# An exp without its wait for the older exp, an early flag and branch hints in a fused attention and FFN kernel

One core of a Trainium2 chip. The metric is the device time of the kernel in microseconds (us), lower is better. All outputs are checked against the reference. Engines: PE is TensorE, DVE VectorE, ACT ScalarE, POOL GpSimd, SP SyncE. A semaphore is what one engine updates and another waits for when a result is ready; the records hold the times of its updates. "The kernel before" and "the changed kernel" are the two versions compared.

## The reference

Multi-query attention (32 heads of 16, one K and V for all) on a normalized input, times a gate made by an FFN, plus the input. S = 2048, D = 512, F = 1792, bfloat16.

```python
xn = _layernorm(x, axis=-1)
# A: q = xn@wq (32 heads), k = xn@wk, v = xn@wv
scores = jnp.einsum("bhqd,bkd->bhqk", q, k) * (Dh ** -0.5)
p = _softmax(scores, axis=-1)
s = (jnp.einsum("bhqk,bkd->bhqd", p, v) ...) @ wo
# B:
g = _silu((_silu(xn @ w_gate) * (xn @ w_up)) @ w_down)
return x + s * g
```

## The kernel before

The body is a static schedule. PE makes a 128x1024 tile of scores into one of three PSUM buffers (`ring`). The exp is taken by ACT for most of the tiles and by DVE, in several operations, for the others; PE multiplies the result with V. ACT writes its exps into eight buffers `Pb` in turn. The exp written into a buffer now must come after the products that read its former content, and these come after the exp that wrote it:

```python
    NPB = 8
    Pb = [sb([P, 1024], BF16, f"Pb{i}") for i in range(NPB)]
    # ... (cut)
    def act_sc(i, b, x, start, dur=MMF):
        # ... (cut: places the score products sc of this tile, and picks k, the number of the exp)
            buf = Pb[k % NPB][:]
        ex = OP("ACT", 0.904, [sc, pb_rel[k - NPB] if k >= NPB else None, cur["exp"]],
                lambda: nc.scalar.activation(out=buf, in_=ring[i][:], func=ACT.Exp, scale=escale, bias=ebias),
                (1,), name="exp")
        # ... (cut: pb_rel[k] becomes the product on PE that reads the buffer)
```

The kernel takes the softmax without a maximum. At the end it tests whether all denominators lay in range; if not, a branch computes everything again by an exact path. With ordinary data the branch skips that path (it is taken). The end of the kernel, with the last four row tiles of the output:

```python
    tadd("DVE", e_out_mul(LN, obk[0], dsts[0]))
    fin_add(0, nc.gpsimd, "POOL")
    # ... (cut: three more products and additions)
    for k in range(4):
        tadd("SP", e_out_st(LN + k))
    tadd("DVE", nc.vector.tensor_reduce(out=fmin[:, 2:3], in_=dlc[:], axis=AX.X, op=ALU.min))
    tadd("DVE", nc.vector.tensor_reduce(out=fmin[:, 3:4], in_=fmin[:, 0:3], axis=AX.X, op=ALU.min))
    tadd("PE", nc.tensor.matmul(out=tq01[0:1, 0:1], lhsT=fmin[:, 3:4], rhs=ones_f[:], start=True, stop=True))
    tadd("DVE", nc.vector.tensor_single_scalar(out=flag_i[:], in_=tq01[0:1, 0:1], scalar=P - 0.5, op=ALU.is_lt))
    MAIN.close()

    flag = nc.values_load(flag_i[0:1, 0:1], min_val=0, max_val=1)
    with tc.If(flag > 0):
        _exact_max_path(...)
```

`tadd(engine, instruction)` appends to the order of an engine. `values_load` loads the flag into a register of every engine, because every engine branches (the trace has five loads of 472 to 539 ns, at 775.05 to 775.06 us, and five branches).

Of the kernel before, what the change touches and what calls it, by code (L numbers as in the profile page):

```python
# [13 lines left out]
ACT = mybir.ActivationFunctionType  # L14
ALU = mybir.AluOpType
AX = mybir.AxisListType
# [3 lines left out]
P = 128  # L20
# [263 lines left out]
def kernel(  # L284
# [13 lines left out]
    nc = tc.nc  # L298
# [8 lines left out]
    escale = LN2 / GRID  # L307
    ebias = -COFF * LN2
# [18 lines left out]
    flag_i = const.tile([1, 1], I32, name="flag_i")  # L327
# [22 lines left out]
    def sb(shape, dtype, name):  # L350
        return wp.tile(shape, dtype, name=name)

    ring = [psum.tile([P, 1024], FP32, name=f"ring{i}") for i in range(3)]
# [20 lines left out]
    NPB = 8  # L374
# [17 lines left out]
    dlc = sb([P, 32], FP32, "dlc")  # L392
    fmin = sb([P, 4], FP32, "fmin")
    ones_f = sb([P, 1], FP32, "ones_f")
# [3 lines left out]
    _last = {}  # L398

    def chain(eng, ins):  # L400
        for bi in (ins if isinstance(ins, (list, tuple)) else [ins]):
            if eng in _last:
                tc.add_manual_dep(bi.ins, _last[eng].ins.name, _nosync, reason="order")
            _last[eng] = bi
# [8 lines left out]
    for c in range(1, NSC):  # L413
# [12 lines left out]
                                        in_=wk_sb[:].rearrange("p k (o d) -> p k o d", o=1).to_broadcast(  # L426
                                            [P, KC, 8, DH])))
# [4 lines left out]
    for i in range(NWARM):  # L432
        chain("PE", nc.tensor.matmul(out=ring[2][:, 512:1024], lhsT=ident_bf[:], rhs=QB[1][:],  # L433
                                     start=True, stop=True))
# [52 lines left out]
    def cmm(dst, w, rhs, start, stop):  # L487
        return [nc.tensor.matmul(out=dst[GRP * j:GRP * j + GRP, :], lhsT=w[:, GRP * j:GRP * j + GRP], rhs=rhs,  # L488
                                 start=start, stop=stop, tile_position=(0, GRP * j)) for j in range(P // GRP)]
# [4 lines left out]
    def OP(eng, dur, deps, emit, prio, mode=None, name=""):  # L494
        return sd.new(_Op(eng, dur, deps, emit, prio, mode, name))
# [118 lines left out]
    for c in range(1, NSC):  # L614
# [4 lines left out]
                name="kev")  # L619
# [62 lines left out]
    def e_out_mm(n, dst, jjs):  # L682
        qs, tt = n // 4, n % 4
        r = []
        for jj in jjs:
            r += cmm(dst, oT[qs % 2][:, jj, tt * P:(tt + 1) * P], wo_sb[:, jj, :], jj == 0, jj == NQ - 1)
        return r

    def e_out_mul(n, src, dst):
        return nc.vector.scalar_tensor_tensor(out=dst[:, :D], in0=src, scalar=0.25, in1=g2_sb[:, n, :],  # L690
                                              op0=ALU.mult, op1=ALU.mult)

    def e_out_add(n, src, eng):
        r = res[n % 4]
        return eng.tensor_tensor(out=r[:, :D], in0=src[:, :D], in1=x_sb[:, n, :] if n >= LN else r[:, :D], op=ALU.add)

    def e_out_st(n):
        return nc.sync.dma_start(out=out_v[:, n, :], in_=res[n % 4][:, :D])
# [39 lines left out]
    def pv_emit(b, mms):  # L738
        for (_, _, g) in mms:
            pv_total[(b, g)] = pv_total.get((b, g), 0) + 1  # L740

        def f():
            r = []
            for (lhs, rhs, g) in mms:
                n = first_pv.get((b, g), 0)
                first_pv[(b, g)] = n + 1
                r.append(nc.tensor.matmul(out=o_ps[GRP * g:GRP * g + GRP, :], lhsT=lhs, rhs=rhs,  # L747
                                          start=(n == 0), stop=(n == pv_total[(b, g)] - 1),
                                          tile_position=(0, GRP * g)))
            return r  # L750
        return f
# [35 lines left out]
    cur = {"ba": 0, "lastx": 1, "nA": 0, "exp": None, "pair": None, "np": 0, "issued": 0, "lastsc": None, "junk": 0, "nX": 0, "pa": None}  # L787
    slot = [None, None, None]
    pb_rel = []
# [30 lines left out]
    def act_block():  # L820
        b = cur["ba"]
        while b < NBLK and rem(b, 0) + rem(b, 1) == 0:
            b += 1
        return b if b < NBLK else None
# [58 lines left out]
    def mm_of(lhs_of, buf, t, half, gs):  # L883
        return [(lhs_of[:, t, DH * half:DH * half + GRP], buf(g), g) for g in gs]
# [14 lines left out]
    def check_done(b):  # L899
        if nx[b][0] == NT and nx[b][1] == NT and not (cur["pair"] is not None and cur["pair"][0] == b):  # L900
            assert not unp[b][0] and not unp[b][1]
            fin_b.add(b)
            kb_ready[b] = cur["lastsc"]
            finish_block(b)

    def place_sc(sl, b, x, start, dur):
        ensure_open(b)
        t = take(b, x)
        ks = k_ready[t // 4][b % 2]
        ks = ks[t % 4 // 2:t % 4 // 2 + 1] if len(ks) > 1 else ks  # L910
        sc = _Op("PE", dur, [slot[sl]] + ks + q_ready[b // 2], sc_emit(sl, b, t, x), (0,), "r", "sc")
        sc.seq = sd.seq
        sd.seq += 1
        sd.place(sc, start)
        cur["lastsc"] = sc
        return sc, t

    act_q = []

    def act_sc(i, b, x, start, dur=MMF):  # L920
        sc, t = place_sc(i, b, x, start, dur)
        cur["lastx"] = x
        pre = b == 1 and cur["ba"] == 0 and act_block() == 0
        if pre:
            k = -1 - cur["nX"]
            buf = XB[cur["nX"]]
            cur["nX"] += 1
        else:
            cur["ba"] = b
            k = cur["nA"]  # L930
            cur["nA"] += 1
            buf = Pb[k % NPB][:]
            pb_rel.append(None)
        if k >= NPB:
            assert pb_rel[k - NPB] is not None
        ex = OP("ACT", 0.904, [sc, pb_rel[k - NPB] if k >= NPB else None, cur["exp"]],
                lambda: nc.scalar.activation(out=buf, in_=ring[i][:], func=ACT.Exp, scale=escale, bias=ebias),  # L937
                (1,), name="exp")
        cur["exp"] = ex
        act_q.append(ex)  # L940
        if len(act_q) > 8:
            act_q.pop(0)
        slot[i] = ex
        unp[b][x].append((ex, k, t, buf))
        if unp[b][0] and unp[b][1]:
            half = b % 2
            mms, dps, ks = [], [], []
            for xx in range(2):
                e_, k_, t_, b_ = unp[b][xx].pop(0)
                mms += mm_of(VA, lambda g, b_=b_: b_[:, (g % 2) * 512:(g % 2 + 1) * 512], t_, half,  # L950
                             (2 * xx, 2 * xx + 1))
                dps += [e_, v_ready[t_ // 4][0]]
                ks.append(k_)
            pv = OP("PE", MMF, dps + [oev[b - 1]], pv_emit(b, mms), (1, b, min(ks)), "c", "pv")
            blk_pv[b].append(pv)
            for k_ in ks:
                if k_ >= 0:
                    pb_rel[k_] = pv
        check_done(b)
        return sc  # L960
# [265 lines left out]
    def pe_do(start, what):  # L1226
# [44 lines left out]
        if dt is None:  # L1271
            act_sc(i, b, act_x(b), start)
            return
# [42 lines left out]
    def tadd(eng, ins):  # L1316
        chain(eng, ins)
# [4 lines left out]
    tq01, tq23 = ring[lb][:, 0:512], o_ps[:]  # L1322
# [14 lines left out]
    dlf = dl[:].rearrange("p h q g o -> p (h q g o)")  # L1337
    tadd("DVE", nc.vector.tensor_scalar(out=dlc[:], in0=dlf, scalar1=DEN_LO, scalar2=DEN_HI, op0=ALU.max, op1=ALU.min))
    tadd("DVE", nc.vector.tensor_tensor(out=dlc[:], in0=dlc[:], in1=dlf, op=ALU.is_equal))
    dsts = [ab[0], ab[1], oa[(LB + 1) % 4], oa[(LB + 2) % 4]]  # L1340
    obk = [bank[k][:, :D] for k in st["obank"]]
    for k in range(2):
        tadd("PE", e_out_mm(LN + k, obk[k], [NQ - 1]))
    for k in range(2, 4):
        tadd("PE", e_out_mm(LN + k, obk[k], [NQ - 1]))

    def fin_add(k, eng, nm):
        tadd(nm, e_out_add(LN + k, dsts[k], eng))

    tadd("DVE", e_out_mul(LN, obk[0], dsts[0]))  # L1350
    fin_add(0, nc.gpsimd, "POOL")
    tadd("DVE", e_out_mul(LN + 1, obk[1], dsts[1]))
    tadd("DVE", e_out_mul(LN + 2, obk[2], dsts[2]))
# [3 lines left out]
    fin_add(3, nc.vector, "DVE")  # L1357
    for k in range(4):
        tadd("SP", e_out_st(LN + k))
    tadd("DVE", nc.vector.tensor_reduce(out=fmin[:, 2:3], in_=dlc[:], axis=AX.X, op=ALU.min))  # L1360
    tadd("DVE", nc.vector.tensor_reduce(out=fmin[:, 3:4], in_=fmin[:, 0:3], axis=AX.X, op=ALU.min))
    tadd("PE", nc.tensor.matmul(out=tq01[0:1, 0:1], lhsT=fmin[:, 3:4], rhs=ones_f[:], start=True, stop=True))
    tadd("DVE", nc.vector.tensor_single_scalar(out=flag_i[:], in_=tq01[0:1, 0:1], scalar=P - 0.5, op=ALU.is_lt))
    MAIN.close()


    flag = nc.values_load(flag_i[0:1, 0:1], min_val=0, max_val=1)
    with tc.If(flag > 0):
        _exact_max_path(tc, nc, wo_sb, x_v, out_v, wq_sb, xnT, KT, VA, g2_sb, ident_bf, ident_f, qscale,
                        S, D, H, NT, NQ, NSC, HD)  # L1370

# [29 lines left out]
```

## Time and profile before

| | kernel before |
|---|---|
| median of 3 runs | 783.76 us (783.62 to 784.1) |
| profiled span | 780.9 us, 21436 instructions |
| granted TensorE clock, mean share of full speed | 0.994 |
| last store issued / landed | 774.27 / 775.98 us |
| end of the records | 780.93 us |

The span is the stretch that has records. The measured time is longer, here by 1.8 to 3.4 us; no record shows what fills the rest. In the groups of instructions (line, engine, operation, tile, shape, count | busy us, mean ns of one | idle time of the engine just before and what ended most of it), this is the exp:

```profile
L937 ACT ACTIVATE Pb<-ring 128x1024 bf16<-128x1024 f32 x772 | 726.4, 1141 | 2.5 <-PE ring L877 2.3
```

The 772 exps fill 726.4 of 780.9 us, and ACT was idle before them for only 2.5 us in all. Their mean is 1141 ns.

### The profile page before, as it was taken

The page shows a single profiled execution, that of the slowest core. Times are in us where ns is not written, and L with a number is a line of the kernel's source. Part 1 is how long each engine was busy: PE and PEld are TensorE (multiplying, and loading weights), DVE is VectorE, ACT ScalarE, POOL GpSimd, SP SyncE. Part 2 cuts the span into 40 slices and gives each one's busy share as a digit, 9 for nine tenths or more (in the row PEclk, how much of TensorE's full clock was granted, in tenths as well). Part 3 has the DMA queues.
Part 4 walks back from the last instruction along what each step waited for, and adds up shares of the span by engine and source line. Part 5 has one row for each costly group of instructions (what it writes and reads, how often), then busy time and mean ns, then how long its engine had stood idle before and what let it go on. Part 6 is the DMA issues. An engine that isn't in the chain of part 4 may idle for free.

```text
span 780.9 us, 21436 instructions
## 1 busy us (share of the span) xinstructions
PE 749.8 (96%) x9095; PEld 230.2 (29%) x9095; DVE 735.7 (94%) x920; ACT 757.2 (97%) x866; POOL 53.5 (7%) x59
## 2 busy tenths in 40 slices
PE   8999999999999999999999999999999999999994
PEld 3323223322222333322232322222223333222221
DVE  7689999999999999999999999999999999999994
ACT  6999999999999999999999999999999999999992
POOL 2100000000012000000001110000000300000101
PEclk9999999999999999999999999999999999999997
DMA  9400000000001000000000100000000000000001
GB/s 329 139 8 9 16 2 24 2 8 17 6 27 49 24 2 8 17 2 24 3 10 29 42 23 2 24 1 9 17 2 24 29 22 2 3 23 2 23 2 32
DMA packets 21199, 20.20 MB, mean 26 GB/s; under 512 B 8744, under 2 KB 17192, under 8 KB 21096
## 3 DMA queue, kind: packets, MB, share of 16 engines
q1 hardware_dynamic: 19512, 18.20, 7.7%
q8 instruction: 73, 1.20, 0.6%
q10 hardware_dynamic: 1584, 0.56, 0.3%
q14 instruction: 30, 0.25, 0.1%
HBM read 14.19 MB, written 2.34 MB: 21 GB/s over the span
## 4 chain that ended last, share of the span: by engine, by line
PE 46%; ACT 38%; issue 8%; DVE 6%; SPq 0%; DMA 0%; ACTq 0%; POOL 0%; DVEq 0%; POOLq 0%
ACT Pb L937 33%; PE ring L877 17%; PE m_ps L488 15%; PE o_ps L747 13%; ACT th L657 3%; DVE Bf L991 2%; ACT g_sb L937 1%; DVE Bf L1010 1%; PE ring L433 1%; ACT th L674 1%; DVE x_sb L1010 0%; DVE x_sb L1005 0%; PE ring L488 0%; DVE hT L663 0%; DVE Bf L1005 0%
## 5 line engine op out<-in xcount | busy, mean ns | idle before, releaser
L937 ACT ACTIVATE Pb<-ring 128x1024 bf16<-128x1024 f32 x772 | 726.4, 1141 | 2.5 <-PE ring L877 2.3
L877 PE MATMUL ring<-QB,KT 32*128 32x512 bf16 x2048 | 306.1, 382 | 15.5 <-ACT Pb L937 8.9
L991 DVE TENSOR_SCALAR Bf<-ring 128x1024 uint16<-128x1024 f32 x172 | 209.6, 1218 | 5.4 <-PE ring L877 4.0
L877 PEld LDWEIGHTS <-KT 32*128 32x128 bf16 x2048 | 94.4, 91 | 314.1 <-issue 307.4
L747 PE MATMUL o_ps<-Pb,VA 128*32 128x512 bf16 x1544 | 146.9, 385 | 0.0
L1010 DVE TENSOR_TENSOR Bf<-Bf,Bf 128x2048 f16<-128x2048 f16 x74 | 90.3, 1220 | 0.1
L991 DVE TENSOR_SCALAR x_sb<-ring 128x1024 uint16<-128x1024 f32 x72 | 87.7, 1218 | 2.5 <-PE ring L877 2.1
L747 PE MATMUL o_ps<-xnT,zw 128*32 128x512 bf16 x1092 | 83.1, 381 | 0.0
L488 PE MATMUL m_ps<-xnT,wu_sb 128*32 128x512 bf16 x896 | 72.6, 384 | 0.8 <-DVE ab L659 0.6
L488 PE MATMUL m_ps<-wd_sb,hT 128*32 128x512 bf16 x896 | 71.5, 383 | 0.1
L488 PE MATMUL m_ps<-xnT,wg_sb 128*32 128x512 bf16 x896 | 70.4, 384 | 0.0
L747 PE MATMUL o_ps<-Bf,VD 128*32 128x512 f16 x688 | 67.1, 385 | 0.9 <-DVE Bf L1010 0.5
L732 POOL TENSOR_TENSOR oT<-oa,rb 128x512 bf16<-128x512 f32 x15 | 22.0, 1464 | 615.6 <-DMA rb<-dscr 409.2
L1017 DVE TENSOR_SCALAR Bf<-Bf 128x2048 uint16<-128x2048 uint16 x86 | 62.0, 721 | 0.6
L747 PEld LDWEIGHTS <-VA 128*32 128x32 bf16 x1560 | 38.0, 94 | 53.8 <-issue 51.5
L1005 DVE TENSOR_SCALAR Bf<-Bf 128x2048 uint16<-128x2048 uint16 x74 | 51.2, 700 | 0.0
L659 DVE SCALAR_TENSOR_TENSOR ab<-th,m_ps 128x512 f32<-128x512 f32 x56 | 38.1, 681 | 4.2 <-ACT th L657 3.9
L657 ACT ACTIVATE th<-m_ps 128x512 f32<-128x512 f32 x56 | 40.1, 716 | 0.0
L663 DVE TENSOR_TENSOR hT<-ab,m_ps 128x512 bf16<-128x512 f32 x56 | 38.2, 682 | 2.0 <-PE m_ps L488 1.6
L747 PEld LDWEIGHTS <-VD 128*32 128x32 f16 x976 | 26.5, 94 | 39.4 <-issue 35.8
L747 PEld LDWEIGHTS <-zw 128*32 128x32 bf16 x1092 | 25.8, 95 | 25.5 <-issue 12.9
L1010 DVE TENSOR_TENSOR x_sb<-x_sb 128x2048 f16<-128x2048 f16 x24 | 29.2, 1217 | 0.0
(121 smaller groups left out, 416.3 us busy)
## 6 DMA issues: line engine op xcount, KB each, us to landing
rb<-dscr SPq DMA_DIRECT2D x15, 256.0 KB
out_dram<-xn SPq DMA_DIRECT2D x16, 128.0 KB, 1.9
dn<-oa SPq DMA_DIRECT2D x120, 2.0 KB, 1.7
oa<-oa SPq DMA_DIRECT2D x60, 32.0 KB, 2.0
wg_sb<-in_B_w_gate_dram SPq DMA_DIRECT2D x1, 1792.0 KB, 11.5
wu_sb<-in_B_w_up_dram SPq DMA_DIRECT2D x1, 1792.0 KB
wd_sb<-in_B_w_down_dram SPq DMA_DIRECT2D x1, 1792.0 KB, 20.3
x_sb<-in_A_x_dram SPq DMA_DIRECT2D x3, 512.0 KB
```

Of the source, the lines that this page charges most:

```text
L488: return [nc.tensor.matmul(out=dst[GRP * j:GRP * j + GRP, :], lhsT=w[:, GRP * j:GRP * j + GRP], rhs=rhs, start=start, stop=stop, tile_posi ...
L657: t_ = OP("ACT", 0.477, [a], lambda: nc.scalar.activation(out=th[i][:], in_=m_ps[:], func=ACT.Tanh, scale=0.5), (0,), name="tanh")
L659: s_ = OP("DVE", 0.6, [t_, ab_rel[i]], lambda: nc.vector.scalar_tensor_tensor(out=ab[i][:], in0=th[i][:], scalar=1.0, in1=m_ps[:], op0=ALU ...
L663: h = OP("DVE", 0.6, [b], lambda: nc.vector.tensor_tensor(out=hT[:, f, :], in0=ab[i][:], in1=m_ps[:], op=ALU.mult), (1,), name="hmul")
L732: return [pk, q], lambda eng: eng.tensor_tensor(out=oT[qs % 2][:, jj, :], in0=o0[:], in1=rbt[:], op=ALU.mult)
L747: r.append(nc.tensor.matmul(out=o_ps[GRP * g:GRP * g + GRP, :], lhsT=lhs, rhs=rhs, start=(n == 0), stop=(n == pv_total[(b, g)] - 1), tile_ ...
L877: return lambda: [nc.tensor.matmul(out=ring[sl][:, u * 512:(u + 1) * 512], lhsT=KT[half][GRP * g:GRP * g + GRP, t * P:(t + 1) * P], rhs=QB ...
L937: lambda: nc.scalar.activation(out=buf, in_=ring[i][:], func=ACT.Exp, scale=escale, bias=ebias),
L991: lambda: nc.vector.tensor_scalar(out=U[:, hs], in0=ring[si][:], scalar1=ubias, scalar2=UINF, op0=ALU.add, op1=ALU.min), (1.5, u), name="p ...
L1005: o1 = OP("DVE", 0.6, [pa, pa0] + wrel, lambda: nc.vector.tensor_scalar(out=Bf[wi], in0=U, scalar1=0x3FF, scalar2=0x3800, op0=ALU.bitwise_and,
L1010: return lambda: eng.tensor_tensor(out=Bf[wi][:, a:z].bitcast(FP16), in0=Bf[wi][:, a:z].bitcast(FP16), in1=U[:, a:z].bitcast(FP16), op=ALU ...
L1017: o2 = OP("DVE", 0.6, o3, lambda: nc.vector.tensor_scalar(out=U, in0=U, scalar1=0x7C00, scalar2=None, op0=ALU.bitwise_and), (2, u, 1), nam ...
```

## The change

Three parts. (a) An exp is no longer told to wait for the exp eight earlier, because its wait for the products on PE implies it. (b) The flag is computed and loaded before the last output products, not after the last store. (c) Each engine gets a branch hint ahead of the closing branch. In the kernel before, ACT, DVE, PE and SP go on only 2.7 to 4.1 us after their branches, and four instruction fetches (three of 8 KB, one of 16 KB, at 776.5 to 776.9 us) lie in that stretch; the hope was that a hint brings such fetches forward.

```diff
-        ex = OP("ACT", 0.904, [sc, pb_rel[k - NPB] if k >= NPB else None, cur["exp"]],
-                lambda: nc.scalar.activation(out=buf, in_=ring[i][:], func=ACT.Exp, scale=escale, bias=ebias),
-                (1,), name="exp")
+        def emit():
+            bi = nc.scalar.activation(out=buf, in_=ring[i][:], func=ACT.Exp, scale=escale, bias=ebias)
+            if k >= NPB:
+                tc.declare_no_dep(bi.ins, exp_ins[k - NPB].ins,
+                                  reason="waits for the products on PE that read the older exp's output")
+            if k >= 0:
+                exp_ins[k] = bi
+            return bi
+        ex = OP("ACT", 0.904, [sc, pb_rel[k - NPB] if k >= NPB else None, cur["exp"]], emit, (1,), name="exp")
 ... (cut: the two reductions and the flag's product move ahead of the last output products)
     tadd("DVE", e_out_mul(LN, obk[0], dsts[0]))
+    tadd("DVE", nc.vector.tensor_single_scalar(out=flag_i[:], in_=tq01[0:1, 0:1], scalar=P - 0.5, op=ALU.is_lt))
+    for en, et in (("SP", "SP"), ("POOL", "Pool"), ("PE", "PE"), ("DVE", "DVE"), ("ACT", "Activation")):
+        with tc.issue_after(_last[en].ins):
+            tc.mark_branch_hint_location("exact", "LikelyTaken", [getattr(mybir.EngineType, et)])
+    loads, vals = nc.values_load_multi_w_load_instructions(flag_i[0:1, 0:1])
+    flag = vals[0]
+    tadd("SP", [l for l in loads if l.ins.engine == nc.sync.engine])
     fin_add(0, nc.gpsimd, "POOL")
 ...
-    flag = nc.values_load(flag_i[0:1, 0:1], min_val=0, max_val=1)
-    with tc.If(flag > 0):
+    with tc.If(flag > 0, label="exact"):
```

The new load of the flag has no bounds, so the two instructions that test them on SP (FUSED_REGOPS, SEQ_ASSERT) are gone as well.

More of the change, by code (lines that the diff above doesn't have):

```diff
@@ L916, in place_sc @@
         return sc, t
-    act_q = []
+    act_q, exp_ins = [], {}
     def act_sc(i, b, x, start, dur=MMF):
@@ L1339 @@
     tadd("DVE", nc.vector.tensor_tensor(out=dlc[:], in0=dlc[:], in1=dlf, op=ALU.is_equal))
+    tadd("DVE", nc.vector.tensor_reduce(out=fmin[:, 2:3], in_=dlc[:], axis=AX.X, op=ALU.min))
+    tadd("DVE", nc.vector.tensor_reduce(out=fmin[:, 3:4], in_=fmin[:, 0:3], axis=AX.X, op=ALU.min))
     dsts = [ab[0], ab[1], oa[(LB + 1) % 4], oa[(LB + 2) % 4]]
@@ L1343 @@
         tadd("PE", e_out_mm(LN + k, obk[k], [NQ - 1]))
+    tadd("PE", nc.tensor.matmul(out=tq01[0:1, 0:1], lhsT=fmin[:, 3:4], rhs=ones_f[:], start=True, stop=True))
     for k in range(2, 4):
@@ L1359 @@
         tadd("SP", e_out_st(LN + k))
-    tadd("DVE", nc.vector.tensor_reduce(out=fmin[:, 2:3], in_=dlc[:], axis=AX.X, op=ALU.min))
-    tadd("DVE", nc.vector.tensor_reduce(out=fmin[:, 3:4], in_=fmin[:, 0:3], axis=AX.X, op=ALU.min))
-    tadd("PE", nc.tensor.matmul(out=tq01[0:1, 0:1], lhsT=fmin[:, 3:4], rhs=ones_f[:], start=True, stop=True))
-    tadd("DVE", nc.vector.tensor_single_scalar(out=flag_i[:], in_=tq01[0:1, 0:1], scalar=P - 0.5, op=ALU.is_lt))
     MAIN.close()
-    flag = nc.values_load(flag_i[0:1, 0:1], min_val=0, max_val=1)
-    with tc.If(flag > 0):
+    with tc.If(flag > 0, label="exact"):
         _exact_max_path(tc, nc, wo_sb, x_v, out_v, wq_sb, xnT, KT, VA, g2_sb, ident_bf, ident_f, qscale,
```

## The prediction

> **What bounds the kernel now.** I read the busy table, the chain that ended last, the line view of the exp, the chain piece by piece at one place in the middle and at the end, and the line view of the closing branch.
>
> ```profile
> PE 749.8 (96%) x9095; PEld 230.2 (29%) x9095; DVE 735.7 (94%) x920; ACT 757.2 (97%) x866; POOL 53.5 (7%) x59
> PE 46%; ACT 38%; issue 8%; DVE 6%; SPq 0%; DMA 0%; ACTq 0%; POOL 0%; DVEq 0%; POOLq 0%
> ```
>
> Three engines are nearly full, and the chain changes between PE (46%) and ACT (38%): no one engine is the bound for long. In the stretch from 115 to 715 us ACT is busy 99.6 to 100% of each 100 us, PE about 97 to 98%, DVE 96 to 98%. What can be won inside the body is therefore not work but the latency with which one full engine hands over to the other.
>
> ```profile
> L937 ACT ACTIVATE Pb<-ring x772: 1017/1134/1316, 12.9 to 765.1; 128x1024 bf16<-128x1024 f32 x193
> L937 ACTq EVENT_SEMAPHORE  x735: 17/17/17, 12.1 to 764.9; - x184
> ```
>
> This is the line of the exp (count, shortest/median/longest ns). Nearly each exp has an EVENT_SEMAPHORE of its own in the ACT sequencer. The compiled order says why: 733 exps wait for two semaphores, PE (their scores) and ACT itself (the exp eight earlier that wrote the same Pb buffer). In the records PE's wait is in the separate instruction and ACT's own in the exp.
>
> ```profile
> 61.47 0.04 issue
> 61.52 0.82 ACT Pb L937
> 62.34 0.10 issue
> 62.44 0.70 ACT Pb L937
> ```
>
> In these pieces of the chain (start, length, what) the exp of 61.52 follows ACT's own work by the chain's account. By the records it was late: PE's semaphore rose at 61.434 and it started 83 ns later, 987 ns after the exp before, where 904 is the undisturbed pitch. So the chain hides a wait for PE under ACT and issue.
>
> ```profile
> L1368 ACTq COMPARE_BRANCH  x1: 50/50/50, 775.6 to 775.6; - x1
> L1368 PEldq COMPARE_BRANCH  x1: 4038/4038/4038, 775.7 to 775.7; - x1
> L1368 SPq COMPARE_BRANCH  x1: 50/50/50, 776.2 to 776.2; - x1
> L1368 ACTq EVENT_SEMAPHORE  x1: 17/17/17, 778.4 to 778.4; - x1
> L1368 SPq EVENT_SEMAPHORE  x8: 17/17/17, 779.0 to 779.5; - x8
> ```
>
> ```profile
> 773.31 0.93 DVE xn L695
> 774.24 0.11 DVE fmin L1360
> 774.37 0.17 DVE fmin L1361
> 774.58 0.20 PE ring L1362 x2
> 774.88 0.15 DVE flag_i L1363
> ```
>
> The last five lines are the chain's end: it stops at 775.03, but the span is 780.93. The 5.9 us after it have no engine work. In the line of the branch (the five lines above) all engines take the branch at 775.6 to 776.2, and the next instruction comes 2.8 us later on ACT (778.40), 2.7 on SP (778.99) and 4.0 on PE, whose branch itself is recorded as 4038 ns. The DMA records show instruction fetches in between: three of 8 KB and one of 16 KB between 776.5 and 776.9.
>
> [...]
>
> **The change part by part.**
>
> *(a) The exp's own wait.* By the order of instructions, 764 exps afterwards wait for PE alone, so the PE wait moves into the exp and the separate instruction goes. The cost is in the sums of the records: of 116 exps between 13 and 768 us that started more than 18 ns late against the pitch, those with two waits start 82 to 83 ns after PE's semaphore rises; the five ACT instructions that waited for PE with one wait only (at 8.0, 10.3, 12.1, 32.9 and 383.8 us) start 22 to 23 ns after it. The difference is 60 ns. An exp that is not late gains nothing: the pitch is 904 ns with two waits (400 us) and with one (14 to 24 us) alike. Taking for each of the 116 the smaller of 60 ns and its lateness gives 5.9 us. How much of it reaches the end? A saving adds to the next one only where PE in between waits for ACT; otherwise PE keeps its own time and ACT merely waits longer at the next place. About 330 score products start 41 to 42 ns after ACT's semaphore with PE idle before, and between the 116 late exps there is such a wait 110 times. Walking through both lists and letting each engine advance by no more than it waited gives 5.4 us. This is a ceiling: it ignores waits that just do not bind now, above all those of DVE, which is 96 to 98% busy and has its own turns on the chain (6%). I take two thirds, 3.6 us. Against it: 31 more tanh (60 instead of 29) now carry ACT's own wait, because the exp no longer implies it, so PE's wait goes to a separate instruction there. No tanh is among the late ones, so I count 0 for this.
>
> *(b) The flag early.* The two reductions (0.172 and 0.156 us, 0.206 apart) move ahead of the first output product on DVE. They fit before it: dlc ends at 769.51, two reductions bring it to 769.93, and the first product waits for PE until 770.14 anyway. The tiny flag product goes into PE's gap around 770.1. Only the flag operation (0.146 us, about 0.17 with its turn) enters DVE's row of products and additions, so the last addition ends at 774.41 instead of 774.24 and the last store is issued at about 774.44 instead of 774.265. In return nothing comes after it: the reductions, flag product, flag, register load and SP's two assertion instructions (774.24 to 776.24 before) are done by 771.5 on the engines that are idle by then.
>
> *(c) The hints.* If the target page is there when SP branches, at 774.44 + 0.34 (issue) + 0.05, SP is at its final waits by about 774.95. It then waits for the last store, which landed 1.71 us after its issue (775.976): 776.15. From SP's second final wait (779.085), where that store is checked, to the end took 1.85 us (15 more waits of 60 to 70 ns each and two rounds of barrier). 776.15 + 1.85 = 778.0 against 780.93: 2.9 us saved. PE's fetch of 4.0 us starts by 771.6 at the latest and is done by 775.7 even without a hint.
>
> Sum: 3.6 + 2.9 = 6.5; with a discount for a hint that does not work, 6.2 us: 777.5.
>
> **The rivals.** *The hints do nothing.* Then SP branches at 774.85, loses 2.75 us as before, and ends at about 777.6 + 1.95 = 779.5: the tail gives 1.4 us, the whole about 778.9. For it: no trace here has a hint. Against: the change puts one on each engine well ahead of the branch, over 2.8 us ahead on SP. *The waits save nothing, because PE or DVE is the real bound.* For it: PE is packed with filler products and DVE is 97% full, and a late exp may only mirror a late PE. Against: the 330 places where PE waits for ACT. It would leave 2.9 us: 780.9. [...] *The new flag steps delay the output products more*, by PE's tiny product waiting for DVE or ACT: some tenths of a microsecond.
>
> **Range and chances.** The tail has 2.9, less likely 1.4 or 0; the waits 1.5 to 5.4. Low: 783.76 - 2.9 - 5.2 = 775.7. High: 783.76 - 1.4 - 2.2 = 780.2. 2% is 15.7 us, beyond the sum of both ceilings (8.3), and nothing added is worth 15 us: 97% within 2%, 2% faster, 1% slower.
>
> **What would show it.** The exp's line has almost no EVENT_SEMAPHORE left, late exps start 22 to 23 ns after PE's semaphore, and the exp's pitch stays 904. The sum of lateness on ACT falls by 2 to 5 us, and the start of the closing output products moves earlier by about 3.6 us. After the last store SP's first final wait follows within some 0.2 us, and last store to end is about 3.5 us instead of 6.7. I am wrong in (a) if the output products start at the same time as before, or more than 5.4 us earlier; wrong in (c) if 2.7 us still lie between SP's branch and its next instruction.

## The result

The changed kernel took 781.86 us (median of 6 fast runs, 780.73 to 782.44), the kernel before 783.49 us in the same rounds (783.19 to 784.1). The ratio is 0.9975 with an interval of 0.9962 to 0.9988: faster by a quarter of a per cent. Ratios here compare fast runs of the same rounds and lie within 0.0002 of the ratio of their means, so they are not quite the ratio of the medians that are quoted. The time lies above the predicted range.

The busy table and the chain of the changed kernel, shares by engine:

```profile
span 780.0 us, 20705 instructions
PE 748.7 (96%) x9095; PEld 229.3 (29%) x9095; DVE 733.8 (94%) x920; ACT 757.0 (97%) x866; POOL 53.7 (7%) x59
PE 47%; ACT 44%; DVE 6%; issue 1%; POOL 0%; SPq 0%; DMA 0%; ACTq 0%; DVEq 0%; POOLq 0%
```

731 instructions are gone. In the chain "issue" went from 8% to 1%, as one would wish, but ACT went from 38% to 44%: the time was renamed, not removed. The busy times are those of before. The exp's line, in the line view and in the groups:

```profile
L937 ACT ACTIVATE Pb<-ring x772: 1017/1206/1376, 12.7 to 764.2; 128x1024 bf16<-128x1024 f32 x193
L937 ACTq EVENT_SEMAPHORE  x2: 17/17/17, 11.8 to 12.7; - x2
```

```profile
L937 ACT ACTIVATE Pb<-ring 128x1024 bf16<-128x1024 f32 x772 | 730.8, 1202 | 2.2 <-PE ring L877 2.1
```

The separate wait instructions went from 735 to 2, as predicted; those of the 72 tanh stayed at 72. The mean exp grew by 61 ns, from 1141 to 1202. That is about the 60 ns by which a late exp now starts sooner after PE's semaphore: **nearly all of them start earlier and end when they did.** The last exp starts at 764.2 instead of 765.1, and 0.22 of this is the first exp, whose start varies from 12.56 to 13.06 us over all the traces.

The closing branch and the final waits (sequencer instructions by engine):

```profile
L1378 SPq EVENT_SEMAPHORE  x8: 17/17/17, 777.4 to 778.6; - x8
L1378 ACTq COMPARE_BRANCH  x1: 68/68/68, 770.6 to 770.6; - x1
L1378 PEldq COMPARE_BRANCH  x1: 3845/3845/3845, 770.7 to 770.7; - x1
...
L1378 ACTq EVENT_SEMAPHORE  x1: 17/17/17, 773.4 to 773.4; - x1
...
L1378 SPq COMPARE_BRANCH  x1: 70/70/70, 774.9 to 774.9; - x1
```

ACT, DVE, PE and SP still stall after their branches: ACT from 770.62 to 773.37, PE 3.9 us, SP from 774.87 to 777.39, 2.5 us. The hints gave nothing here. And something new is in the line of the final stores (16 stores in the kernel, shortest/median/longest ns of the issue on SP), before first, then changed:

```profile
L698 SPq DMA_DIRECT2D out_dram<-xn x16: 332/346/869, 232.6 to 774.3; - x16
...
DMA to landing us min/median/max: 1.7/1.9/2.2
```

```profile
L698 SPq DMA_DIRECT2D out_dram<-xn x16: 332/352/1527, 232.1 to 774.0; - x16
...
DMA to landing us min/median/max: 1.7/1.9/2.9
```

The issue of 1527 ns is that of the second of the last four stores (343 ns before); the fourth took 842 (332 before). So the last store was issued 0.57 us after its data was ready, where it was 0.03 before. It also landed later: the last of its 16 completion updates, for which SP waits, comes at 778.18, 4.2 us after the issue, against 1.71 before. Fifteen of the 16 had come by 776.38; before, all came from 775.81 to 775.98. (The view's landing figures leave this store out: of the last four they pair only the first and the third.)

The records account for 0.90 us of the gain, from 780.93 to 780.03:

| | before | changed | difference |
|---|---|---|---|
| start to first output product on DVE | 770.14 | 769.31 | -0.83 |
| first output product to end of the last addition on DVE | 4.10 | 4.11 | 0 |
| last addition to issue of the last store | 0.03 | 0.57 | +0.54 |
| issue of the last store to the end | 6.67 | 6.05 | -0.62 |

The rest is outside the records. In its six runs the changed kernel's measured time exceeds the span by 1.82 to 1.88 us (1.77 in a repeat further down); in the kernel before by 1.8 to 3.4, with means of 2.54, 2.64 and 2.79 in three sets of nine runs. So some 0.7 to 1.0 us of the measured gain is time that no record shows. The experiments come back to it.

### The profile page after: what moved, and what is told of

Same layout as the page of the kernel before. It is cut to its first block, busy times and chain, and to the rows that moved or that the text cites. A ratio compares the mean times of both kernels' runs of the same rounds, so it can differ in the third digit from the quotient of the medians.

```text
span 780.0 us, 20705 instructions
## 1 busy us (share of the span) xinstructions
PE 748.7 (96%) x9095; PEld 229.3 (29%) x9095; DVE 733.8 (94%) x920; ACT 757.0 (97%) x866; POOL 53.7 (7%) x59
## 4 chain that ended last, share of the span: by engine, by line
PE 47%; ACT 44%; DVE 6%; issue 1%; POOL 0%; SPq 0%; DMA 0%; ACTq 0%; DVEq 0%; POOLq 0%
ACT Pb L937 40%; PE ring L877 17%; PE m_ps L488 16%; PE o_ps L747 13%; ACT th L657 3%; DVE Bf L997 1%; ACT g_sb L937 1%; DVE Bf L1016 1%; ACT th L674 1%; DVE x_sb L997 0%; DVE Bf L1023 0%; PE ring L488 0%; DVE hT L663 0%; DVE Bf L1011 0%; DVE x_sb L1011 0%
## 5 line engine op out<-in xcount | busy, mean ns | idle before, releaser
L657 ACT ACTIVATE th<-m_ps 128x512 f32<-128x512 f32 x56 | 43.7, 781 | 0.0
```

What stands on the lines that cost most here:

```text
L657: t_ = OP("ACT", 0.477, [a], lambda: nc.scalar.activation(out=th[i][:], in_=m_ps[:], func=ACT.Tanh, scale=0.5), (0,), name="tanh")
```

## The experiments

Nine new kernels ran, and two repeats: four, four and three at a time, each set beside nine runs of the kernel before. All runs but the two single repeats, whose state is unknown, were in the fast state (granted clock 0.994 to 0.998). By the 2% line every one is "same"; what can be told apart is in the intervals. This table collects the tail of each, read from the trace of its profiled run, in us. "Stall" is from the branch to the engine's next instruction. "Outside" is the measured time less the span, the mean of the timed runs.

| kernel | last store issued | longest of the 4 issues | landing after issue | stall ACT / DVE / PE / SP | end | outside |
|---|---|---|---|---|---|---|
| before | 774.27 | 0.34 | 1.71 | 2.81 / 3.13 / 4.10 / 2.74 | 780.93 | 2.5 to 2.8 |
| changed | 773.98 | 1.53 | 4.2 | 2.75 / 3.24 / 3.90 / 2.52 | 780.03 | 1.84 |
| wait only | 773.34 | 0.34 | 1.71 | 3.24 / 3.24 / 4.04 / 2.80 | 780.06 | 2.54 |
| tail only | 774.31 | 0.35 | 3.3 | 2.59 / 3.76 / 2.21 / 3.29 | 779.91 | 1.84 |
| no hints | 774.14 | 1.52 | 4.1 | 2.78 / 3.24 / 3.83 / 2.66 | 780.12 | 1.87 |
| early hints | 773.68 | 0.65 | 2.57 | 0.49 / 0.62 / 0.48 / 0.95 | 778.09 | 1.85 |
| shorter exp | 764.80 | 1.15 | 2.4 | 2.61 / 2.99 / 3.52 / 2.60 | 769.76 | 1.81 |
| no branch | 773.75 | 0.34 | 1.71 | none | 776.91 | 2.10 |
| late flag, early hints | 773.16 | 0.34 | 1.71 | 0.49 / 0.63 / 0.48 / 2.85 | 779.96 | 1.77 |
| hold | 773.15 | 0.34 | 1.70 | 0.48 / 0.63 / 0.48 / 0.51 | 777.25 | 1.85 |
| late flag, no bounds check | 773.76 | 0.34 | 1.71 | 0.48 / 0.63 / 0.48 / 0.51 | 777.53 | 1.83 |
| changed, again | 774.33 | 1.58 | 3.6 | 2.72 / 2.87 / 4.01 / 2.65 | 779.77 | 1.77 |
| tail only, again | 774.39 | 1.38 | 3.8 | 2.57 / 2.98 / 3.74 / 2.52 | 780.07 | 1.76 |

### The exp's wait alone

The kernel before, with the exp's part of the diff above and nothing else.

> The kernel before with only the exp's own wait taken away. Theory A (new, from the two traces: the ends of successive exps lie 916 to 917 ns apart whether the start was late or not, so a late start is overlap given up and not time lost): at most 0.8 us faster, about 0.5 us; the exps start earlier after PE's semaphore (22 to 23 ns instead of 82) and last about 60 ns longer, ends still 917 apart. Rival B (the prediction: each late start is lost time): 3 to 5 us faster.

Measured: 782.75 us against 783.41, ratio 0.9995 with an interval of 0.9981 to 1.0009, which includes 1. In the records, from the end of the first exp to the first output product it took 755.44 us against 756.19: 0.75 less. Over all traces this stretch took 756.14 to 756.21 us in the three with the wait and 755.36 to 756.03 in the nine without it (full exps): 0.6 less in the mean, 0.1 to 0.85 in single pairs. So the wait is worth some 0.6 us of the body, not 3.6. A direct view of why is a row of five exps in both kernels (from the records; us, and durations in ns; numbered by ACT's instructions from the first exp on, tanh included):

```
            before                                   changed
exp   start    after last start  dur   end after   start    after last start  dur   end after
437   398.579        905        1180     918       397.922        904        1297     917
438   399.483        904        1192     916       398.826        904        1309     916
439   400.467        984        1126     918       399.865       1039        1187     917
440   401.388        921        1121     916       400.786        921        1182     916
441   402.292        904        1133     916       401.690        904        1195     917
```

("End after" is the time from the end of the exp before.) Exp 439 **started** late by 80 ns before and 135 ns afterwards, and **ended** 918 and 917 ns after its predecessor, like all the others. The durations carry the answer: with each start 904 ns and each end 916 to 917 ns after the last, an exp's record grows by 12 ns from one to the next, so the starts run ahead of the ends. In the kernel before, exp 439 started 208 ns before the end of 438, in the changed kernel 270 ns. A late start only uses up this lead. 98% of the exps' ends lie 914 to 919 ns after the end before them (99% in the changed kernel), whatever the starts did.

Counted by ends, 10 exps of the kernel before were late by over 6 ns, 2.98 us in all; in the changed kernel 7, with 2.36 us. Exp by exp, the three latest lost 57 to 62 ns each, four lost 19 to 179, and three kept their lateness within 3 ns: those gained nothing from the change. Counted by starts it was 116 before and 120 after, with lateness of 11.1 and 10.6 us: a number that hardly moves, because it does not measure loss.

### The tail alone

The changed kernel with the old exp, so parts (b) and (c).

> The changed kernel with the exp's own wait put back: flag early and hints alone. Theory A: nearly the whole gain stays, 1 to 1.7 us faster than before. Rival B: the early flag alone gains nothing or costs something, and the wait's removal gave it all: within 0.3 us of before. The last stores should again be disturbed by instruction fetches, last store issued to end about 6 us.

Measured: 781.86 against 783.41, ratio 0.9985 (0.9971 to 0.9998). From the end of the first exp to the first output product it took 756.15 us, the value of before, which confirms that the body's gain is the exp's wait. The span is shorter by 0.6 us in the mean of the runs (780.14 against 780.74) and the part outside by 0.7. The stores were issued without delay, yet the last landed 3.3 us after its issue. PE stalled 2.21 us instead of some 4: in this run a 16 KB instruction fetch stood at 771.19, before PE's branch at 771.55.

### The tail without hints

```diff
-    for en, et in (("SP", "SP"), ("POOL", "Pool"), ("PE", "PE"), ("DVE", "DVE"), ("ACT", "Activation")):
-        with tc.issue_after(_last[en].ins):
-            tc.mark_branch_hint_location("exact", "LikelyTaken", [getattr(mybir.EngineType, et)])
```

> The changed kernel without the five hints. Theory C (hints placed behind the engine's last ordinary fetch start no fetch, as the changed kernel's trace shows none after them): within 0.3 us of the changed kernel, and the same 2.5 to 3.9 us between each engine's branch and its next instruction. Rival D (the hints do shorten the branch a little): 0.5 us or more slower than the changed kernel.

Measured: 781.74 us, ratio 0.9979 (0.9965 to 0.9992), like the changed kernel. The stalls, the store issue of 1.52 us and the late landing are the same. **The hints, where the change puts them, are worth nothing that these runs can tell.** The first one stood at 733.0 on SP, 42 us before its branch, against stalls of 2.5 to 3.9 us, so SP's had time enough. In the changed kernel no instruction fetch stands between the last three hints (768.8 to 769.5) and 771.57, about 1 us after the first branch; after the hints of SP and POOL (733.0, 736.0) there are only three 16 KB fetches, at 741.80, 754.66 and 765.11, which the kernel before has as well (743.26, 755.56 and 766.59).

### The hints placed much earlier

The changed kernel, with each hint moved into the body: SP's to 284 us, POOL's to 84, ACT's to 608, DVE's to 647 and PE's to 758. The choice came from the trace: the last ordinary instruction fetches of the engines lie at about 455 us (SP), 670 (ACT), 702 (DVE) and 765 (PE), and all hints of the change stood after them. (The records of fetches name no engine, so this is the estimate: the 71 fetches of 16 KB in the body have 256 records of PE and its weight loads from one to the next, in the median, and go to PE; those of 8 KB were given to the others by counting instructions.)

```diff
+    hint_at = {"SP": ("SP", 300.0), "POOL": ("Pool", 100.0), "PE": ("PE", 747.0), "DVE": ("DVE", 640.0),
+               "ACT": ("Activation", 600.0)}
     for i, o in enumerate(order):
         ...
+        for en, (et, at) in list(hint_at.items()):
+            if o.start >= at and en in _last:
+                with tc.issue_after(_last[en].ins):
+                    tc.mark_branch_hint_location("exact", "LikelyTaken", [getattr(mybir.EngineType, et)])
+                del hint_at[en]
 (and the hints of the changed kernel taken out)
```

> The changed kernel with each hint moved ahead of the last ordinary instruction fetch of its engine (SP near 300 us, ACT near 610, DVE near 650, PE near 760). Theory C, second part (a hint is honoured together with the next ordinary fetch): the branch stall falls from 2.5 to 3.9 us to some 0.2 us, no fetch falls among the last stores, which then are issued in 0.34 us each and land 1.7 us after issue; the end comes about 2 us earlier than in the changed kernel, about 779.7 us. If hints do nothing here at all: the same as the changed kernel within 0.3 us.

Measured: 780.3 against 783.41, ratio 0.9963 (0.995 to 0.9977). The lines of the branch:

```profile
L1382 SPq EVENT_SEMAPHORE  x8: 17/17/17, 775.0 to 776.7; - x8
L1382 ACTq COMPARE_BRANCH  x1: 68/68/68, 770.7 to 770.7; - x1
L1382 PEldq COMPARE_BRANCH  x1: 420/420/420, 770.7 to 770.7; - x1
L1382 ACTq EVENT_SEMAPHORE  x1: 17/17/17, 771.1 to 771.1; - x1
```

PE's branch takes 420 ns instead of 3845, ACT goes on after 0.49 us instead of 2.75. The same hints, placed before the engine's last ordinary fetch by that estimate, leave stalls of 0.48 to 0.95 us. But the stores are still disturbed (up to 653 ns of issue, landing 2.57 us after issue): four instruction fetches stand between 771.85 and 775.19, among the stores.

### The exp made shorter

The changed kernel with exps over 1008 of the 1024 columns (the rest of the buffer holds ones, the error is 0.107); it asks whether ACT is the bound at all. Its output is wrong, which doesn't matter for the time.

```diff
-            bi = nc.scalar.activation(out=buf, in_=ring[i][:], func=ACT.Exp, scale=escale, bias=ebias)
+            w = 1008 if k >= 0 else 1024
+            bi = nc.scalar.activation(out=buf[:, 0:w], in_=ring[i][:, 0:w], func=ACT.Exp, scale=escale, bias=ebias)
```

> The changed kernel with each exp into a Pb buffer cut from 1024 to 1008 columns (wrong result on purpose; the missing columns are set to 1 once at the start). Theory A (ACT alone is the bound: 780 exps end every 917 ns): the ends come 16/1.2 = 13.3 ns closer by the tempo of 917 ns for 1024 columns and the fixed part seen there, so 772 exps give up to 10.3 us, less where PE or DVE, 97% full, take over; at least 4 us. Rival B (late exps mirror PE's own lateness, hand-overs share the bound): under 2 us, since PE's products come no earlier.

Measured: 771.41 against 783.18, ratio 0.9849 (0.9834 to 0.9864); 11.8 us less than before, some 10.4 less than the changed kernel's 781.86 of another set. The median distance of the ends fell from 917 to 903 ns, and from the first exp's end to the last it took 742.56 us instead of 751.71: 9.15 us less, where 772 exps shorter by 14 ns are 10.8. (Another 1.5 us between the two traces are in the tail, whose stores were less delayed in this one, so the 10.4 overstate it.) So some 85% of the work taken from ACT reaches the end. The account fits: 779 exps of 917 ns and 72 tanh of 490 ns after the first exp are 749.6 us, of the 752.33 (before) and 751.71 (changed) between first and last end. (By these two distances 512 columns more take 427 ns, 0.834 ns each, so 16 columns are 13.3 ns, the figure of the expectation, and 63 ns are fixed.) **One engine was the bound of the body all along**, and only what makes its ends late could be won: the 2.98 us.

### No branch

The changed kernel without the branch, the register loads and the hints; it has no exact path. It is the floor for the tail.

> The changed kernel without the closing branch, the loads of the flag and the hints (right for this data, but it drops the exact path). It gives the floor of the tail: no fetch among the stores, so four stores of 0.34 us each, the last issued 0.9 us after the last but one, landed 1.7 us later, and then some 1.2 to 1.8 us of final waits. Span about 777 us, 3 us less than the changed kernel, if the branch's fetches cost both the stall and the delayed stores; about 777.5 if only the stall.

Measured: 778.8 against 783.18, ratio 0.9942 (0.9929 to 0.9956). The stores are undisturbed, and last issue to end is 3.16 us. So the branch, with the flag's loads, costs at most some 3.5 us of 6.67 in the kernel before.

### The late flag with early hints

The flag where it was before, with its bounds check; the hints early; the exp's wait gone.

> The kernel before with the exp's own wait away and the hints early, but the flag computed and loaded at the end as before. If the hint is what shortens the tail: each engine's stall falls to 0.5 to 1 us, the stores are undisturbed (0.34 us each, landing 1.7 us after issue), end about 778.2, within 0.3 us of the kernel with early flag and early hints. If the early flag carries the gain: within 0.5 us of the kernel with the wait alone away (end about 780).

Measured: 781.86 against 783.18, ratio 0.9984 (0.9971 to 0.9998). Neither expectation was met in full. The stores are undisturbed (1.71 us to landing), ACT, DVE and PE stall 0.49 to 0.63 us, but SP stalls 2.85 us as if it had no hint, and SP is the engine that closes the kernel:

```profile
L1381 SPq EVENT_SEMAPHORE  x8: 17/17/17, 778.0 to 778.6; - x8
...
L1381 SPq COMPARE_BRANCH  x1: 70/70/70, 775.2 to 775.2; - x1
```

The kernel's mean span is 0.4 us shorter than before; the part outside gave the other 0.9.

### Hold: the early flag, the branches after the stores

Early hints and the flag computed early, but ACT, DVE and PE load it only when the last store has landed, and SP's load stands behind the stores.

```diff
+    loads, vals = nc.values_load_multi_w_load_instructions(flag_i[0:1, 0:1])
+    flag = vals[0]
+    landed = mybir.DependencyInfo(mybir.DependencyClass.Sync, mybir.DependencyReason.DATA)
+    for l in loads:
+        if l.ins.engine in (nc.scalar.engine, nc.tensor.engine, nc.vector.engine):
+            tc.add_manual_dep(l.ins, _last["SP"].ins.name, landed, reason="after the last store has landed")
```

> Flag early, hints early, and the flag's loads of ACT, PE and DVE held until the last store has landed, SP's load behind its stores: no fetch may fall among the stores. If fetches delay the stores: stores issued in 0.34 us each, the last landing 1.7 us after issue instead of 2.6, end about 777.2, some 0.8 us earlier than with early hints alone. If the fetches had nothing to do with it: the stores are as slow as before and the end is no earlier, or later by the loads' 0.5 us.

Measured: 779.58 against 783.18, ratio 0.9953 (0.9939 to 0.9967). It has as many instruction fetches among the last 8 us as the early hints alone. DMA traffic from 771 to 779 us by queue (packets, MB, share of 16 engines) and the stores with their median time to landing (of the two that the view pairs), first of the changed kernel, then of the early hints, then of this one:

```profile
q14 instruction: 6, 0.05, 2.1%
q8 instruction: 2, 0.03, 1.8%
...
out_dram<-xn SPq DMA_DIRECT2D x4, 128.0 KB, 2.7
```

```profile
q14 instruction: 3, 0.02, 1.3%
q8 instruction: 1, 0.02, 0.8%
...
out_dram<-xn SPq DMA_DIRECT2D x4, 128.0 KB, 2.6
```

```profile
q14 instruction: 3, 0.02, 1.0%
q8 instruction: 1, 0.02, 0.8%
...
out_dram<-xn SPq DMA_DIRECT2D x4, 128.0 KB, 1.7
```

Four fetches of the same sizes cost the stores 0.9 us of landing in one kernel and nothing in the other. Hold moved the flag's loads and the branches along with them, so this run shows a collision with what the early branches bring; that the fetches are the part that matters is what the repeats below point to.

### The late flag, early hints, no bounds check

As "late flag, early hints", but loaded without bounds, so that SP's two test instructions are gone.

```diff
-    flag = nc.values_load(flag_i[0:1, 0:1], min_val=0, max_val=1)
+    loads, vals = nc.values_load_multi_w_load_instructions(flag_i[0:1, 0:1])
+    flag = vals[0]
```

> As the run with late flag and early hints, but SP's flag loaded without the bounds check (its two instructions FUSED_REGOPS and SEQ_ASSERT stood between load and branch, and SP alone still stalled 2.85 us there). If those two were what spoiled SP's hint: SP's stall is 0.5 to 1 us, the end comes at about 777.3 (2.6 us earlier), timed near 779.6 us; then the early flag itself is worth nothing. If SP's hint needs the early flag for another reason: SP stalls 2.7 to 2.9 us again and the time is within 0.6 us of 781.3 (the assertion's 0.6 us saved).

Measured: 779.33 against 783.61, ratio 0.9946 (0.9932 to 0.9959): the lowest time of a version with all its function, though not told apart from hold (0.9939 to 0.9967). It beats the kernel before in the same rounds, and the changed kernel by comparison across sets: the intervals of the two ratios, 0.9932 to 0.9959 and 0.9962 to 0.9988, do not overlap. SP stalls 0.51 us instead of 2.85:

```profile
L1382 SPq EVENT_SEMAPHORE  x8: 17/17/17, 775.6 to 776.1; - x8
...
L1382 SPq COMPARE_BRANCH  x1: 70/70/70, 775.1 to 775.1; - x1
```

The flag is as late as in the kernel before, and the last store issue to the end takes 3.77 us instead of 6.67. So the early flag is not needed; with the early hints and the late branch the stores are undisturbed (0.34 us of issue at most, 1.71 us to landing) without any hold.

### Two repeats

The changed kernel and the tail alone once more, one run each (state unknown for single runs).

> The changed kernel once more, for its tail: all theories expect the stalls of its first trace (2.5 to 3.9 us on SP, ACT, DVE and PE) and stores delayed by fetches. If a hint this late is honoured now and then, one engine's stall may be shorter, as PE's 2.2 us was in the run of the tail alone.

> The run of the tail alone once more: if PE's late hint was honoured there by chance, PE's stall is 3.8 to 4.1 us this time; if by this program's layout, it is 2.2 us again with a fetch of 16 KB about 1 us after the hint and before the branch.

Measured: 781.57 and 781.86 us. The changed kernel's delay came again (issues of 349, 1575, 355 and 779 ns, landing 3.6 us after issue, stalls 2.65 to 4.01). The tail alone had it now too (second issue 1377 ns), and PE stalled 3.74 us: its stall of 2.21 in the first trace was an accident of that run, not a property of the program.

The two traces of the tail alone are a test by themselves. ACT's load of the flag stands 1.24 us before the first store in both, and the first 8 KB fetch 0.25 and 0.24 us after it. What differs is the first 16 KB fetch: at 771.19, 1.0 us before the first store, in one trace, and at 772.27, 0.16 us before the second store, in the other. The second store's issue took 346 and 1377 ns. So that delay comes with the fetch, not with the loads.

## Why the prediction was wrong

**(a) The exp's wait: right mechanism, mis-sized term, from a wrong reading.** The wait instructions went (735 to 2), late exps start 22 to 24 ns after PE's semaphore instead of 82 to 83, and the start distance of 904 ns stayed; all as predicted. The step that failed is "Taking for each of the 116 the smaller of 60 ns and its lateness gives 5.9 us", with the two thirds of it, 3.6 us. It took a late start for lost time. By ends only 10 exps were late, and the term measures 0.6 us: 2.98 to 2.36 by late ends, 752.33 to 751.71 from first to last end, 0.75 with the wait alone, 0.6 in the mean of all traces. By the prediction's own test ("start at the same time as before, or more than 5.4 us earlier") it was neither; the first output product came 0.83 us earlier, of which 0.22 belongs to the first exp's start. The opening claim, that no one engine is the bound for long, fell with the short exp. The walk through the PE waits could not see this, as it used the same starts. The rival "the waits save nothing, because PE or DVE is the real bound" was near in size but named the wrong engine: it was ACT itself.

**(b) The early flag: right that it was possible, with a cost of 0 in DVE's row.** The prediction charged 0.17 us for the flag operation; from the first product to the end of the last addition it took 4.10 and 4.11 us, so it fitted into slack. "The last store is issued at about 774.44 instead of 774.265", a delay of 0.17, became 0.54 by another cause that the prediction did not have: SP's issues took up to 1.53 us in a stretch with instruction fetches behind the early branches (8 KB at 771.57 and 16 KB at 771.73, just ahead of the slow issue's start at 771.87). The shown part is the comparison of early hints with hold, and the two traces of the tail alone. The prediction moved a stalling event from after the stores into them, and took it for hidden because it asked only whether PE's fetch was done in time, not what else used the DMA then.

**(c) The hints: failed.** The step is "If the target page is there when SP branches" ("page" is the prediction's word; the records show fetches of 8 and 16 KB). By the prediction's test ("if 2.7 us still lie between SP's branch and its next instruction") it is wrong: 2.5 us. The rival "the hints do nothing" was right, and its counter-argument, that SP's hint stood over 2.8 us ahead, was the error: 42 us were not enough, while a place before the estimated last ordinary fetch was (stalls 0.48 to 0.95). With the hints working and the stores undisturbed the tail gives 2.90 us (6.67 to 3.77) in the last version: the 2.9 us of the prediction, to the tenth, but by luck: that kernel has a late flag. The rival's 1.4 us for the tail without hints became 0.62 less 0.54, because the late landing replaced SP's stall as the last wait.

**What nobody predicted: time outside the records.** The measured time less the span is 2.5 to 2.8 us in the mean for the kernel before and the wait alone, and 1.77 to 1.87 for all other versions with a branch. In those two PE leaves the branch last, after a stall of 4 us and only some 1.2 us before the end (779.76 of 780.93; 778.77 of 780.06). In the others it either left it at least 4.3 us before the end or did not stall (0.48 us). No record shows what happens in that time, so the cause stays open. It is some 0.7 us of the changed kernel's gain of 1.6 to 2.0, and most of that of "tail alone" and "late flag, early hints".

**The sum.** Predicted 6.2; measured 1.6 by medians and 2.0 by means. By the records: exp's wait 0.6 instead of 3.6, tail 0.1 (0.62 less 0.54) instead of 2.9, plus 0.2 by the start; outside the records some 0.7 to 1.0. The prediction had named 0 for the tail and 1.5 for the waits as possible, which together give 782.3; its range left that corner out. Of its smaller sums, 783.76 less 6.2 is 777.56, not 777.5, and 14 final waits, not 15, follow SP's second; neither matters.

Open: why a hint must stand where it worked (with the early hints the number of fetches in the span fell from 97 to 92, four of the five between 771 and 779 us; what a hint does to a fetch was not shown); why two test instructions between load and branch undid SP's hint, or whether it was only where the code then lay; what let PE's fetch run early once; and why two of the changed kernel's six runs took 780.73 and 780.84 us (not by the hints, since a run without them took 780.5).

## What to carry to other kernels

Where a saturated engine's records overlap, measure the distance of its ends, not of its starts; a late start with a normal end has cost nothing (exp 439 started 80 and 135 ns late and ended 918 and 917 ns after the one before). A hint for a branch is judged by the stall behind the branch: of the two places tried here, the one after the engine's last ordinary instruction fetch (by estimate) left stalls of 2.5 to 3.9 us in the changed kernel, the one before it 0.48 to 0.95 us, but 2.85 us on SP where two test instructions stood between load and branch. Moving the branch itself earlier can put its fetches among the last stores: here a store's issue grew from 0.34 to 1.53 us, and the last landing from 1.71 to 4.2 us. Test the bound of a stage by making its suspected engine 1.5% shorter before adding up waits (here 9.15 us of 10.8 reached the last exp's end).
